# A GEGLU feed-forward kernel: x block 1 by DMA transpose instead of TensorE, the early weights issued by ScalarE, a shorter warm-up, and another split of the first bank copies

## The chip, the core and the metric

The kernel runs on one core of a Trainium2 chip. The metric is the device time of one execution in microseconds (us). An execution is timed from outside; the span of a profile is 1.3 to 1.6 us shorter. One core is used, so there is no second die to compare with.

## The reference

```python
B, S, D, F = 32, 32, 1024, 3584          # 1024 rows of x, bf16
out = (gelu_tanh(x @ w_gate) * (x @ w_up)) @ w_down
```

## The kernel before

The bulk of the kernel is a Strassen-like arrangement of 128x512 matmuls, in a stream that TensorE runs almost without a break (busy 268.2 of 270.8 us). The change touches only the first 16 us, where the first eight tiles of h = gelu(x wg) * (x wu) are made for the first 512 rows of x. That stage works in *blocks* of 128 rows of the contraction (block 0 to 7). For the first four tiles ("quad 0") it does blocks 0 and 1, then moves the eight half-done PSUM banks away (`kept`), does the second four tiles ("quad 1"), and comes back. j = 0 is the gate weight, j = 1 the up weight. (The DMAs load x and the weights into SBUF. A PSUM bank takes the 128x512 sums that a row of matmuls adds up; the kernel reuses it once VectorE or ScalarE has copied it out. In the trace of before the last of these copies on VectorE ends at 10.43 us, and its bank is reused at 10.55.)

The kernel holds x transposed in SBUF (`xT`). Blocks 0 and 1 are loaded as they are (`xn`) and transposed on TensorE. Blocks 2 to 7 come by transposing DMAs from SyncE.

```python
for n in [512] * 6 + [P] * 2:                       # warm-up on constants
    mm(3, one[:, 0:P], one[:, 0:n], True, True)
NX = 2
for i, eng in enumerate(("sp", "act")):             # x blocks 0 and 1, as they are
    dma(eng, xn[:, 2*i:2*i+2, :], x_r[:, 2*i:2*i+2, 0:NX*P], 0, f"xn{i}")
# ... load_quad(eng, q, j, k0, k1): weight blocks k0..k1 of quad q, half j
for q in range(2):
    for k in range(NX):
        load_quad("sp", q, 0, k, k + 1)
        load_quad("act", q, 1, k, k + 1)
for k0, k1 in ((2, 3), (3, 4), (4, 5), (5, 6), (6, 8)):
    pr.add("sp", "dma_start_transpose", xT[0][:, k0:k1, :], xf[0:512, k0*P:k1*P], ...)
for k in range(2, 4):
    for j in range(2):
        load_quad("act", 1, j, k, k + 1)
act(warm[:, 0:1], const0, GELU, 0)                  # makes ScalarE load its table
for k in range(NX):                                 # TensorE transposes, VectorE copies out
    ...
for k in range(NX):                                 # quad 0, blocks 0 and 1: matmuls 0 to 15
    for j in range(2):
        for m in range(4):
            raw(m, j, k, 2*m + j, k == 0)           # bank 2m+j
            if k == NX - 1:
                copy(("act", "dve")[m % 2], kept[m][:, j, :], bank(2*m + j), ...)
for i, k in enumerate((4, 6)):                      # blocks 4..7 of quad 1, after those copies
    for j in range(2):
        load_quad("act", 1, j, k, k + 2, 9 + i)
# ... matmuls 16 on: quad 1, blocks 0 to 5, each block 4 gate then 4 up matmuls
```

Below, *matmul n* is the n-th matmul on real data. Matmul 0 is block 0, matmul 8 block 1, matmul 16 the first of quad 1, which reuses the bank of matmul 8; matmul 48 begins block 4 of quad 1.

Of the kernel before, what the change touches and what calls it, by code (L numbers as in the profile page):

```python
# [6 lines left out]
P = 128  # L7
BF16 = mybir.dt.bfloat16
# [115 lines left out]
def bass_standalone__geglu_ffn__sampling_kernel(  # L124
# [11 lines left out]
    DK, FM = D // P, F // P  # L136
# [3 lines left out]
    x_r = xf.rearrange("(tc p) d -> p tc d", p=P)  # L140
# [3 lines left out]
    pr = _Program()  # L144

    with ExitStack() as es:
        def sb(name, shape, dtype):
            return es.enter_context(nc.sbuf_tensor(name, shape, dtype))

        hT = sb("hT", [P, FM, N], BF16)  # L150
# [5 lines left out]
        ident = sb("ident", [P, P], BF16)  # L156
        warm = sb("warm", [P, 2], FP32)
        p1 = sb("p1", [P, 512], FP32)
        ps = es.enter_context(nc.psum_tensor("ps", [P, 8, 512], FP32))
        const0 = nc.const_aps.tensor(0.0, [P, 1], FP32)  # L160

        xT = [arena[:, a:a + 4096].rearrange("p (k n) -> p k n", n=512) for a in (16384, 0)]
        quad = [arena[:, a:a + 8192].rearrange("p (j k c) -> p j k c", j=2, k=DK) for a in (20480, 8192)]
        def duo(a): return arena[:, a:a + 4096].rearrange("p (j k c) -> p j k c", j=2, k=DK)
        wd = [[arena[:, a:a + 7168].rearrange("p (k n) -> p k n", n=512) for a in row] for row in ((0, 7168), (14336, 21504))]
        xn = hT[:, FM - 1, :].rearrange("p (t c) -> p t c", c=2 * P)
        Sf = S[:, :, :].bitcast(FP32)
        Tf = T[:, :, :, :, :].bitcast(FP32)
        T2r = T[:, :, :, :, :].rearrange("p u j k c -> p (u j k c)").rearrange("p (s n) -> p s n", n=512)
# [9 lines left out]
        def mm(bank, lhsT, rhs, start, stop, held=False, add=False):  # L179
            return pr.add("pe", held_matmul if held else "matmul", ps[:, bank, 0:rhs.shape[-1]], lhsT, rhs,  # L180
                          start=start, stop=stop, skip_group_check=add)
# [4 lines left out]
        def act(out, a, f, at):  # L186
            return pr.add("act", "activation", out, a, f, at=at)

        def dma(eng, out, a, at, name, after=()):
            return pr.add(eng, "dma_start", out, a, at=at, dma=name, after=after)  # L190
# [6 lines left out]
        pr.add("pool", "memset", ident[:, :], 0.0)  # L197
        pr.add("pool", "affine_select", ident[:, :], ident[:, :], [[-1, P]], ALU.not_equal, 1.0,
               base=0, channel_multiplier=1)
        for n in [512] * 6 + [P] * 2:  # L200
            mm(3, one[:, 0:P], one[:, 0:n], True, True)

        NX = 2
        for i, eng in enumerate(("sp", "act")):
            dma(eng, xn[:, 2 * i:2 * i + 2, :], x_r[:, 2 * i:2 * i + 2, 0:NX * P], 0, f"xn{i}")

        def load_quad(eng, q, j, k0, k1, at=0, after=()):
            dma(eng, quad[q][:, j, k0:k1, :], w_r[j][:, k0:k1, 4 * q * P:4 * (q + 1) * P], at, f"w{q}_{j}_{k0}", after)

        for q in range(2):  # L210
            for k in range(NX):
                load_quad("sp", q, 0, k, k + 1)
                load_quad("act", q, 1, k, k + 1)
        for k0, k1 in ((2, 3), (3, 4), (4, 5), (5, 6), (6, 8)):
            pr.add("sp", "dma_start_transpose", xT[0][:, k0:k1, :], xf[0:512, k0 * P:k1 * P], dma=f"x{k0}_0")
        for k in range(2, 4):
            for j in range(2):
                load_quad("act", 1, j, k, k + 1)
        act(warm[:, 0:1], const0, GELU, 0)
        for k in range(NX):  # L220
            for i, b in enumerate((6, 7) if k == 0 else (4, 5)):
                half = ps[:, b, 0:P].bitcast(BF16)
                for t in range(2):
                    pr.add("pe", "transpose", half[:, t * P:(t + 1) * P], xn[:, 2 * i + t, k * P:(k + 1) * P], ident[:, :])
                pr.add("dve", "tensor_copy", xT[0][:, k, i * 256:(i + 1) * 256], half)



# [3 lines left out]
        def piece(a): return a.rearrange("p t n -> p (t n)").bitcast(FP32).rearrange("p (j n) -> p j n", j=2)  # L232
        kept = [piece(hT[:, m:m + 2, :]) for m in (14, 16, 18, 20, 22, 24, 26, 10, 12)] + [piece(o11[:, :, :])]
# [10 lines left out]
        bank = lambda b: ps[:, b, :]  # L244

        def copy(eng, out, a, at):
            if eng == "act":
                act(out, a, COPY, at)
            else:
                pr.add("dve", "tensor_copy", out, a, at=at)  # L250
# [3 lines left out]
        def raw(m, j, k, b, start):  # L254
            return mm(b, quad[m // 4][:, j, k, m % 4 * P:(m % 4 + 1) * P], x0[:, k, :], start, k in (NX - 1, 3, DK - 1), add=not start and k >= NX)
# [6 lines left out]
        for k in range(NX):  # L262
            for j in range(2):
                for m in range(4):
                    raw(m, j, k, 2 * m + j, k == 0)
                    if k == NX - 1:
                        copy(("act", "dve")[m % 2], kept[m][:, j, :], bank(2 * m + j), 6.5 + 0.9 * j + 0.1 * m)
        for i, k in enumerate((4, 6)):
            for j in range(2):
                load_quad("act", 1, j, k, k + 2, 9 + i)  # L270
# [376 lines left out]
```

## Time and profile before

| what | where it is read | value |
|---|---|---|
| median time | timed runs | 272.03 us (271.36 to 272.37) at first, 272.09 with three more |
| TensorE busy, span | page, part 1 | 268.2 of 270.8 us |
| first matmul on data | timeline | 4.61 us |
| spacing of matmuls of 512 columns | trace, start to start | 0.427 us until 6.67 us, 0.216 us after |
| last of the bank copies on VectorE ends | trace | 10.43 us, its bank is reused at 10.55 |

The chain of waits of before, in order of time (start, length, what; the count after x is of instructions):

```profile
by line: PE ps L117 99.0%; DVE o L117 0.1%; issue 0.0%
...
0.77 3.79 PE ps L117 x16
4.56 0.05 issue
4.61 264.41 PE ps L117 x1190
```

TensorE bounds the kernel from 0.77 to 269.02 us. Until then nothing else is on the chain for more than 0.05 us, and after it only a last VectorE instruction of 0.29 us. So a change to the start is worth what it does to the TensorE stream and nothing more.

The timeline of TensorE's weight loads in before shows two rates. "The clock switches" means in this document that the spacing of the matmuls falls from 0.427 to 0.216 us. That a clock does it is my reading and not shown: the clock column of the windows view is 1.00 on both sides (before, 4 to 6 and 8 to 10 us). At the slow rate every load stands on a line of its own, 0.43 us apart; at full rate they merge into one line (start, length, engine, source line, operation, tiles, shape, count, idle time before and what ended it):

```profile
3.39 0.90 PEld L117 LDWEIGHTS ps<-ident,hT 128*128 128x128 bf16 x8
4.58 0.14 PEld L117 LDWEIGHTS ps<-arena 128*128 128x128 bf16 x2 [0.29 <-issue]
4.99 0.15 PEld L117 LDWEIGHTS ps<-arena 128*128 128x128 bf16 x1 [0.28 <-DVE arena L117]
5.42 0.15 PEld L117 LDWEIGHTS ps<-arena 128*128 128x128 bf16 x1 [0.28 <-issue]
5.84 0.15 PEld L117 LDWEIGHTS ps<-arena 128*128 128x128 bf16 x1 [0.28 <-issue]
6.27 0.15 PEld L117 LDWEIGHTS ps<-arena 128*128 128x128 bf16 x1 [0.28 <-issue]
6.67 3.55 PEld L117 LDWEIGHTS ps<-arena 128*128 128x128 bf16 x17 [0.25 <-issue]
10.48 0.38 PEld L117 LDWEIGHTS ps<-arena 128*128 128x128 bf16 x3 [0.27 <-DVE hT L117]
```

The bank copies on VectorE in before, from its timeline. They are four, and two alternate with two on ScalarE in each half:

```profile
7.95 2.48 DVE L117 COPY hT<-ps 128x512 f32<-128x512 f32 x4 [3.06 <-PE ps L117]
```

Four stretches of before in the windows view. The columns are the stretch, its length, the busy time of PE, PEld, DVE, ACT and POOL with their instructions, the granted clock, the DMA engines' busy share and their GB/s:

```profile
18.00:20.00 2.00, 2.00 (x11) 0.88 (x9) 0.00 (x0) 0.00 (x0) 0.00 (x0) 1.00 1.10 349
22.40:23.40 1.00, 1.00 (x6) 0.49 (x5) 0.97 (x3) 1.00 (x3) 0.00 (x0) 1.00 1.28 287
22.40:25.40 3.00, 3.00 (x15) 1.37 (x14) 2.97 (x6) 3.00 (x7) 0.00 (x0) 1.00 1.11 163
8.00:12.00 4.00, 4.00 (x20) 1.80 (x19) 2.43 (x4) 1.79 (x4) 0.00 (x0) 1.00 1.13 202
```

From 18 to 20 us only plain weight loads move data (349 GB/s), and from 8 to 12 us both plain loads and transposing DMAs do (202 GB/s). From 22.4 to 25.4 us only transposing DMAs do: the last plain load before had landed at 22.39, the next was issued at 25.69. They moved 287 GB/s in the first of these three microseconds (DMA share 1.28), 149 in the second (share 1.54) and 52 in the third (share 0.52, so part of that time the engines had nothing to do): 163 over all three.

### The profile page before, as it was taken

The numbers are of one execution on the slowest core, as the hardware profiler recorded it, in microseconds if no ns is written. First come the engines' busy times: TensorE is split into PE (matmuls) and PEld (weight loads), VectorE is DVE, ScalarE is ACT, GpSimd is POOL, SyncE is SP. The second block draws the span as 40 slices with busy tenths as digits, with TensorE's granted clock in tenths as the row PEclk, the third lists the DMA queues.
The fourth block names the chain that finished last, engine by engine and source line by source line (L and its number), as shares of the span: only waits on it lengthen the run. The fifth ranks groups of instructions, "written<-read, shape, count | busy, mean of one in ns | idle before, by whom it ended". The sixth has DMA issues, their size and how long they took to land.

```text
span 270.8 us, 3333 instructions
## 1 busy us (share of the span) xinstructions
PE 268.2 (99%) x1206; PEld 192.6 (71%) x1206; DVE 208.2 (77%) x246; ACT 136.1 (50%) x221; POOL 37.1 (14%) x23
## 2 busy tenths in 40 slices
PE   8999999999999999999999999999999999999997
PEld 4444448888888888888776776674458888888884
DVE  1338998998899889988764739379976999999921
ACT  2339877566756675667455554531220305057452
POOL 1000003123302330233344160000000000000000
DMA  6999970050492002971900070294010000002102
GB/s 205 205 316 204 280 188 4 13 141 0 116 291 60 0 0 80 254 251 51 263 0 0 0 247 27 65 351 129 0 39 19 4 0 0 0 0 80 58 21 97
DMA packets 45024, 27.47 MB, mean 101 GB/s; under 512 B 8656, under 2 KB 45008, under 8 KB 45008
## 3 DMA queue, kind: packets, MB, share of 16 engines
q1 hardware_dynamic: 42496, 25.04, 34.0%
q10 hardware_dynamic: 2512, 2.23, 3.3%
q8 instruction: 9, 0.15, 0.2%
q14 instruction: 7, 0.06, 0.1%
HBM read 23.33 MB, written 2.10 MB: 94 GB/s over the span
## 4 chain that ended last, share of the span: by engine, by line
PE 99%; DVE 0%; issue 0%
PE ps L117 99%; DVE o L117 0%
## 5 line engine op out<-in xcount | busy, mean ns | idle before, releaser
L117 PE MATMUL ps<-S,T 128*128 128x512 f32 x560 | 129.2, 391 | 0.0
L117 PEld LDWEIGHTS ps<-S,T 128*128 128x128 f32 x560 | 105.2, 188 | 22.3
L117 ACT ACTIVATE tmp<-ps 128x512 f32<-128x512 f32 x64 | 38.0, 596 | 51.7 <-PE ps L117 51.5
L117 POOL TENSOR_TENSOR T<-arena 128x1024 fp32r<-128x1024 bf16 x17 | 36.4, 2153 | 124.5 <-PE ps L117 81.7
L117 PE MATMUL ps<-T,S 128*128 128x512 f32 x224 | 51.3, 390 | 0.0
L117 DVE TENSOR_TENSOR T<-arena,T 128x1024 fp32r<-128x1024 bf16 x42 | 51.0, 1220 | 0.2
L117 PEld LDWEIGHTS ps<-T,S 128*128 128x128 f32 x224 | 42.1, 188 | 8.8
L117 ACT ACTIVATE ps<-ps 128x512 f32<-128x512 f32 x44 | 25.6, 584 | 37.0 <-PE ps L117 37.0
L117 DVE TENSOR_TENSOR hT<-tmp,ps 128x512 bf16<-128x512 f32 x56 | 37.0, 684 | 8.7 <-PE ps L117 6.7
L117 PE MATMUL ps<-arena 128*128 128x512 bf16 x192 | 43.5, 385 | 0.1
L117 DVE TENSOR_TENSOR tmp<-ps,tmp 128x512 f32<-128x512 f32 x28 | 19.4, 692 | 23.5 <-PE ps L117 23.5
L117 PEld LDWEIGHTS ps<-arena 128*128 128x128 bf16 x192 | 18.5, 99 | 23.7 <-issue 2.4
L117 DVE TENSOR_TENSOR T<-arena 128x1024 fp32r<-128x1024 bf16 x25 | 30.0, 1222 | 4.4 <-PE ps L117 4.3
L117 DVE TENSOR_TENSOR ps<-ps,tmp 128x512 f32<-128x512 f32 x32 | 22.3, 696 | 3.0 <-PE ps L117 3.0
L117 PE MATMUL ps<-arena,hT 128*128 128x512 bf16 (+2 forms) x126 | 24.6, 356 | 0.0
L117 PEld LDWEIGHTS ps<-arena,hT 128*128 128x128 bf16 x126 | 11.7, 98 | 12.7 <-issue 0.5
L117 ACT ACTIVATE tmp<-tmp 128x512 f32<-128x512 f32 x28 | 17.6, 632 | 2.4 <-DVE tmp L117 2.1
L117 ACT ACTIVATE ps<-hT 128x512 f32<-128x512 f32 x22 | 13.0, 599 | 7.6 <-DVE hT L117 7.6
L117 DVE TENSOR_TENSOR S<-hT 128x1024 fp32r<-128x1024 bf16 x14 | 16.6, 1221 | 0.0
L117 ACT ACTIVATE T<-arena 128x1024 fp32r<-128x1024 bf16 x14 | 14.8, 1059 | 0.0
L117 ACT ACTIVATE hT<-ps 128x512 f32<-128x512 f32 x18 | 9.5, 602 | 7.0 <-PE ps L117 7.0
L117 PE MATMUL ps<-S 128*128 128x512 f32 x56 | 12.9, 389 | 0.0
(33 smaller groups left out, 94.4 us busy)
## 6 DMA issues: line engine op xcount, KB each, us to landing
arena<-in_w_down_dram SPq DMA_DIRECT2D x4, 1792.0 KB, 9.4
arena<-in_w_gate_dram SPq DMA_DIRECT2D x10, 512.0 KB, 4.8
arena<-in_w_up_dram SPq DMA_DIRECT2D x10, 512.0 KB, 5.9
out_dram<-arena SPq DMA_DIRECT2D x12, 128.0 KB, 1.7
arena<-in_w_up_dram ACTq DMA_DIRECT2D x6, 128.0 KB, 5.6
arena<-in_w_gate_dram SPq DMA_DIRECT2D x3, 256.0 KB, 6.3
arena<-in_w_up_dram SPq DMA_DIRECT2D x3, 256.0 KB, 6.5
arena<-in_w_gate_dram SPq DMA_DIRECT2D x4, 128.0 KB, 5.1
```

The source lines that it names most:

```text
L117: ins = name(eng, *args, **kw) if callable(name) else getattr(eng, name)(*args, **kw)
```

## The change

The intent is to begin sooner. TensorE transposes only block 0, so the two x loads halve (64 KB each; they landed in before at 3.25 and 3.46) and four transposes go. Block 1 comes by the first transposing DMA. To make room on SyncE's queue, ScalarE issues nearly all early weights, block by block, gate and up in turn. The warm-up shrinks from six matmuls of 512 columns and two of 128 to five and one. ScalarE is then busy issuing for longer (its last early issue ended at 5.23 in before), so five of the eight bank copies go to VectorE.

```diff
-        for n in [512] * 6 + [P] * 2:
+        for n in [512] * 5 + [P]:
...
-            dma(eng, xn[:, 2 * i:2 * i + 2, :], x_r[:, 2 * i:2 * i + 2, 0:NX * P], 0, f"xn{i}")
+            dma(eng, xn[:, 2 * i:2 * i + 2, :], x_r[:, 2 * i:2 * i + 2, 0:P], 0, f"xn{i}")
...
-        for q in range(2):
-            for k in range(NX):
-                load_quad("sp", q, 0, k, k + 1)
-                load_quad("act", q, 1, k, k + 1)
-        for k0, k1 in ((2, 3), (3, 4), (4, 5), (5, 6), (6, 8)):
+        load_quad("sp", 0, 0, 0, 1)
+        load_quad("act", 0, 1, 0, 1)
+        for q, k0, k1 in ((0, 1, 2), (1, 0, 1), (1, 1, 2), (1, 2, 4)):
+            for j in range(2):
+                load_quad("act", q, j, k0, k1)
+        for k0, k1 in ((1, 2), (2, 3), (3, 4), (4, 5), (5, 6), (6, 8)):
             pr.add("sp", "dma_start_transpose", xT[0][:, k0:k1, :], ...)
-        for k in range(2, 4):
-            for j in range(2):
-                load_quad("act", 1, j, k, k + 1)
...          # the TensorE transposes: block 0 alone, banks 6 and 7
-                        copy(("act", "dve")[m % 2], kept[m][:, j, :], ...)
+                        copy("act" if (m, j) in ((3, 0), (1, 1), (3, 1)) else "dve", kept[m][:, j, :], ...)
```

More of the change, by code (lines that the diff above doesn't have):

```diff
@@ L165, in bass_standalone__geglu_ffn__sampling_kernel @@
         wd = [[arena[:, a:a + 7168].rearrange("p (k n) -> p k n", n=512) for a in row] for row in ((0, 7168), (14336, 21504))]
-        xn = hT[:, FM - 1, :].rearrange("p (t c) -> p t c", c=2 * P)
+        xn = hT[:, FM - 1, 0:4 * P].rearrange("p (t c) -> p t c", c=P)
         Sf = S[:, :, :].bitcast(FP32)
@@ L204, in bass_standalone__geglu_ffn__sampling_kernel @@
         for i, eng in enumerate(("sp", "act")):
-            dma(eng, xn[:, 2 * i:2 * i + 2, :], x_r[:, 2 * i:2 * i + 2, 0:NX * P], 0, f"xn{i}")
+            dma(eng, xn[:, 2 * i:2 * i + 2, :], x_r[:, 2 * i:2 * i + 2, 0:P], 0, f"xn{i}")
         def load_quad(eng, q, j, k0, k1, at=0, after=()):
             dma(eng, quad[q][:, j, k0:k1, :], w_r[j][:, k0:k1, 4 * q * P:4 * (q + 1) * P], at, f"w{q}_{j}_{k0}", after)
-        for q in range(2):
-            for k in range(NX):
-                load_quad("sp", q, 0, k, k + 1)
-                load_quad("act", q, 1, k, k + 1)
-        for k0, k1 in ((2, 3), (3, 4), (4, 5), (5, 6), (6, 8)):
+        load_quad("sp", 0, 0, 0, 1)
[4 more added lines that the diff above has]
+        for k0, k1 in ((1, 2), (2, 3), (3, 4), (4, 5), (5, 6), (6, 8)):
             pr.add("sp", "dma_start_transpose", xT[0][:, k0:k1, :], xf[0:512, k0 * P:k1 * P], dma=f"x{k0}_0")
-        for k in range(2, 4):
-            for j in range(2):
-                load_quad("act", 1, j, k, k + 1)
         act(warm[:, 0:1], const0, GELU, 0)
-        for k in range(NX):
-            for i, b in enumerate((6, 7) if k == 0 else (4, 5)):
-                half = ps[:, b, 0:P].bitcast(BF16)
-                for t in range(2):
-                    pr.add("pe", "transpose", half[:, t * P:(t + 1) * P], xn[:, 2 * i + t, k * P:(k + 1) * P], ident[:, :])
-                pr.add("dve", "tensor_copy", xT[0][:, k, i * 256:(i + 1) * 256], half)
+        for i in range(2):
+            half = ps[:, 6 + i, 0:P].bitcast(BF16)
+            for t in range(2):
+                pr.add("pe", "transpose", half[:, t * P:(t + 1) * P], xn[:, 2 * i + t, :], ident[:, :])
+            pr.add("dve", "tensor_copy", xT[0][:, 0, i * 256:(i + 1) * 256], half)
         NP, EARLY = 14, 10
@@ L266, in bass_standalone__geglu_ffn__sampling_kernel @@
                     if k == NX - 1:
-                        copy(("act", "dve")[m % 2], kept[m][:, j, :], bank(2 * m + j), 6.5 + 0.9 * j + 0.1 * m)
+                        copy("act" if (m, j) in ((3, 0), (1, 1), (3, 1)) else "dve", kept[m][:, j, :], bank(2 * m + j), 6.5 + 0.9 * j + 0.1 * m)
         for i, k in enumerate((4, 6)):
```

## The prediction

> **What bounds the kernel now.** TensorE. The page gives PE 268.2 us of a 270.8 us span, and the chain of waits is PE from 0.77 us to 269.0 us almost without a break. In the timeline, matmuls of 512 columns start every 0.427 us until 6.67 us and every 0.216 us afterwards (the fp32 products of the bulk every 0.226 us). After 6.67 us I find only about 16 gaps, under 2 us together. So the change can touch only what stands before the stream reaches full rate, plus any new gap it makes. [...] no run here shows yet what moves the switch.
>
> **Before, in the timeline.** Warm-up 0.77 to 3.50, eight transposes 3.50 to 4.35 (0.107 each), VectorE copies 3.95 to 4.89 (0.29 each), first real matmul 4.61. Five real matmuls run at the slow rate, the rest at 0.216. Matmul 8 (block 1) starts at 7.32, matmul 16 (second four tiles) at 9.04.
>
> **Removed.** One warm-up matmul of 512 and one of 128 columns (0.53 us), four transposes (0.43 us), two copies. The x pieces halve, so they should land about 0.25 us earlier than 3.25 and 3.46. Block 0 is still bound by x landing, then transpose, then copy: the last transpose at about 3.3, plus the 0.79 us from transpose to matmul seen before, gives a first matmul near 4.08, some 0.5 us earlier. If the clock still switches near 6.6 us, that half microsecond is slow time: worth only about 0.26 us of stream.
>
> **Added: one transposing DMA for block 1.** SyncE issues it at about 1.75 (before, the first such issue took 1.21 us). Block 1 is needed near 7.1. Before, the first one ran from about 6.3 to 10.2 beside weight traffic, the later one alone took about 2 us. From data at about 3.2 that puts landing between 5 and 7.2: mostly hidden; I allow 0.2 us on average.
>
> **Moved: bank copies.** Before, VectorE and ScalarE each empty four banks; on VectorE one takes 0.68 us, started every 0.60 us, the first 0.42 us after its matmul starts. The last ends at 10.43, and its bank is reused at 10.55: no slack. After, VectorE has five, three of them first. Counted from matmul 8: copies end at +1.11, +1.71, +2.30, +2.90, +3.50; their banks are wanted at +1.73, +1.94, +2.16, +2.59, +3.02. So a new wait of about 0.5 us on TensorE around 9 to 10.5 us, all on the critical path.
>
> **Weights.** ScalarE issues the second tiles' blocks earlier in one queue; total bytes are equal. The tightest landing before is block 4 (15.47 against use at 15.95, 0.5 us slack); the same copies release it, so I expect it to hold.
>
> **Sum.** -0.26 (start) +0.5 (bank copies) +0.2 (block 1) = about +0.4: 272.4 us, 80% range 271.4 to 273.6. Faster by over 2%: 0.3%; within 2%: 98.2%; slower by over 2%: 1.5%.
>
> **What would show it.** First matmul on x near 4.1; a gap or rate change at the same 6 to 7 us; the waits view with PE or its weight load waiting for VectorE's bank copies around 9 to 10.5; block 1's landing before about 7; full rate from there to the end with the same gaps.
>
> **What would make it wrong.** The clock switching at another time [...]. Block 1 landing late behind weights. If TensorE waits for w block 1 anyway, the copies' wait hides under that. If the bank copies are no limit, the result is about 271.7.

Two passages are cut from it: a description of how the clock switches, and, from what would make it wrong, the cause and the size that it gave for a switch at another time. No trace or run of this case shows them. Neither is a term of the sum, which stands whole: -0.26 + 0.5 + 0.2 = +0.44, taken as about +0.4 on the 272.03 us of before.

## The result, and the profile after

After: 272.65 us median of 6 runs (272.31 to 273.30). Before, in the same rounds: 272.09 us median of 6. The ratio is 1.0028, 95% interval 1.0010 to 1.0046. A ratio here is the mean time of one kernel's runs over that of the other's runs of the same rounds, so it is not quite the ratio of the medians. The interval lies above 1, so it is slightly slower.

The chain of waits of after. It no longer begins on TensorE:

```profile
by line: PE ps L117 93.3%; DMA arena<-in_w_gate_dram 2.8%; ACTq L117 2.0%; ACT L117 0.5%; ACT hT L117 0.3%; issue 0.2%; DVE o L117 0.1%; ACT warm L117 0.1%
...
6.38 1.28 ACT L117
...
7.88 0.77 ACT hT L117 x2
8.65 7.61 DMA arena<-in_w_gate_dram
16.27 0.05 issue
16.32 253.12 PE ps L117 x1142
```

Read from the bottom: matmul 48 at 16.32 us waited for the gate weights of block 4. These landed at 16.27 after 7.6 us, and were issued at 8.65 by ScalarE, which until then had issued loads, loaded its table (6.38) and copied banks. Before had no such wait.

The weight loads of after:

```profile
3.19 0.15 PEld L117 LDWEIGHTS ps<-ident,hT 128*128 128x128 bf16 x1
4.16 0.13 PEld L117 LDWEIGHTS ps<-arena 128*128 128x128 bf16 x2 [0.82 <-DMA arena<-in_w_gate_dram]
4.56 0.15 PEld L117 LDWEIGHTS ps<-arena 128*128 128x128 bf16 x1 [0.28 <-issue]
4.99 1.01 PEld L117 LDWEIGHTS ps<-arena 128*128 128x128 bf16 x5 [0.28 <-issue]
6.69 1.88 PEld L117 LDWEIGHTS ps<-arena 128*128 128x128 bf16 x10 [0.69 <-issue]
9.08 0.11 PEld L117 LDWEIGHTS ps<-arena 128*128 128x128 bf16 x2 [0.50 <-DVE hT L117]
9.74 0.13 PEld L117 LDWEIGHTS ps<-arena 128*128 128x128 bf16 x2 [0.55 <-issue]
10.27 0.55 PEld L117 LDWEIGHTS ps<-arena 128*128 128x128 bf16 x4 [0.41 <-DVE hT L117]
```

The first matmul came at 4.16 instead of 4.61. In this execution the clock had already switched at 5.2 us. At 6.72 matmul 8 had waited for block 1 of x, which landed at 6.59 (the line names no releaser; the weights of matmul 8 had landed at 4.76). At 9.08, 9.74 and 10.27 stand the waits for banks that VectorE was still emptying (the line at 9.74 names none either; the fourth copy ended at 9.62, and the weights had landed at 7.91). Its copies and the DMA rate in after:

```profile
7.14 3.08 DVE L117 COPY hT<-ps 128x512 f32<-128x512 f32 x5 [3.21 <-PE ps L117]
```

```profile
4.00:12.00 8.00, 7.49 (x30) 2.76 (x31) 3.08 (x5) 2.96 (x5) 0.00 (x0) 1.00 1.16 206
18.00:20.00 2.00, 2.00 (x11) 0.88 (x9) 0.00 (x0) 0.00 (x0) 0.00 (x0) 1.00 1.10 346
```

The starts of the same matmuls in the two traces give the whole account of the two profiled executions (us; the difference is after minus before):

| stretch | before | after | difference | what it is |
|---|---|---|---|---|
| start to matmul 0 | 4.606 | 4.160 | -0.446 | earlier start |
| 0 to 8 | 2.709 | 2.564 | -0.145 | clock switched earlier (-0.536), wait for x block 1 (+0.391) |
| 8 to 16 | 1.726 | 1.723 | 0.00 | |
| 16 to 40 | 5.180 | 5.726 | +0.546 | bank copies: gaps at matmuls 18, 20, 22 |
| 40 to 64 | 5.180 | 5.638 | +0.458 | late weights of block 4: 0.415 at matmul 48 |
| 64 to end | 249.603 | 249.606 | 0.00 | |
| TensorE's end | 269.004 | 269.417 | +0.413 | |

The wait of 0.391 is the 0.607 us from matmul 7 to matmul 8, less the regular 0.216.

The rows add up, but they are not separate causes. By the chain, matmul 48 began at 16.32 because block 4 landed at 16.27. Without the gaps of the copies TensorE would have come to matmul 48 half a microsecond sooner and, had the landing stayed the same, waited half a microsecond longer there. So in this execution the copies were not on the chain that set the end, although the prediction has their wait "all on the critical path".

One trace is one execution, though. The moment of the clock's switch differs by several microseconds between the profiled executions (full rate from 4.12 us or sooner in k11, from 10.26 in k4), so the experiments were timed as well.

### The profile page after: what moved, and what is told of

It reads as the page before. It is cut to its first block, busy times and chain, and to the rows that moved or that the text cites. A ratio compares the mean times of both kernels' runs of the same rounds, so it can differ in the third digit from the quotient of the medians.

```text
span 271.2 us, 3318 instructions
## 1 busy us (share of the span) xinstructions
PE 267.5 (99%) x1200; PEld 191.3 (71%) x1200; DVE 208.4 (77%) x245; ACT 135.6 (50%) x220; POOL 37.1 (14%) x23
## 4 chain that ended last, share of the span: by engine, by line
PE 93%; DMA 3%; ACTq 2%; ACT 1%; issue 0%; DVE 0%
PE ps L117 93%; DMA arena<-in_w_gate_dram 3%; ACTq L117 2%; ACT L117 0%; ACT hT L117 0%; DVE o L117 0%; ACT warm L117 0%
## 5 line engine op out<-in xcount | busy, mean ns | idle before, releaser
L117 PEld LDWEIGHTS ps<-arena 128*128 128x128 bf16 x192 | 17.9, 98 | 25.6 <-issue 2.8
```

The costliest lines, as they stand in the source:

```text
L117: ins = name(eng, *args, **kw) if callable(name) else getattr(eng, name)(*args, **kw)
```

## The experiments

Theory at the outset: the change starts TensorE 0.45 us sooner; the five serial copies on VectorE take 0.5 us back; waits for data and for the clock take the rest. Rivals: the gaps at 18 to 22 are late data whoever copies; the clock's moment has nothing to do with TensorE's idle time; block 1 of x alone is the cause.

A summary first. "Full rate from" is the first matmul start at the 0.216 us spacing in the one profiled execution. The waits are the gaps beyond the regular spacing in that execution. The kernel before was run 42 more times beside them, on four chips: 271.32 to 272.41 us, medians 271.60 to 271.87.

| run | median us (range) | ratio to before (95%) | full rate from | waits of TensorE in its trace |
|---|---|---|---|---|
| before | 272.09 (271.36 to 272.37) | | 6.67 | none |
| after | 272.65 (272.31 to 273.30) | 1.0028 (1.0010, 1.0046) | 5.25 | x block 1 0.39, copies 0.5, block 4 0.42 |
| k1 even copies | 272.38 (271.96 to 273.23) | 1.0024 (1.0007, 1.0041) | 6.87 | up weights of block 2 0.29 |
| k2 before, split copies | 272.36 (271.89 to 272.93) | 1.0018 (1.0005, 1.0031) | 5.01 | copies 0.5 |
| k3 block 4 early | 272.42 (271.91 to 272.82) | 1.0019 (1.0007, 1.0031) | 4.97 | x block 1 1.21, copies 0.5 |
| k4 even copies, table early | 273.04 (272.16 to 273.92) | 1.0037 (1.0014, 1.0060) | 10.26 | none |
| k5 after, filler | 272.53 (272.08 to 272.67) | 1.0029 (1.0015, 1.0043) | 5.61 | x block 1 0.12, copies 0.5, block 4 0.1 |
| k6 before, block 1 turned late | 272.04 (271.93 to 272.23) | 1.0011 (0.9997, 1.0025) | never | see below |
| k7 warm-up of 3 | 273.00 (272.72 to 273.11) | 1.0044 (1.0030, 1.0059) | 8.66 | copies 0.2 |
| k8 even copies, filler | 272.47 (271.74 to 272.86) | 1.0022 (1.0006, 1.0039) | 6.51 | none |
| k9 even, filler, table early | 272.06 (271.39 to 272.55) | 1.0013 (0.9998, 1.0029) | 5.62 | up weights of block 2 0.39 |
| k10 before, short warm-up | 272.28 (271.64 to 273.33) | 1.0020 (1.0003, 1.0037) | 5.81 | none |
| k11 no wait for x block 1 | 272.26 (271.80 to 273.70) | 1.0024 (1.0005, 1.0044) | 4.12 or sooner | weights 0.33, 0.12, 0.78, copies 0.2 |
| k12 k9 with fine blocks | 272.41 (272.11 to 272.52) | 1.0024 (1.0010, 1.0038) | 6.43 | block 4 0.12 and 0.44 |

For k6 the median, range and ratio are of its four fast executions. All others gave right results; k11 is wrong on purpose. The traces of k5, k6, k7, k8 and k12 lack nine matmul records each; the regular gaps of 0.43 us that this leaves are not counted as waits.

### k1: the even copies put back into after

```diff
-    copy("act" if (m, j) in ((3, 0), (1, 1), (3, 1)) else "dve", kept[m][:, j, :], ...)
+    copy(("act", "dve")[m % 2], kept[m][:, j, :], ...)
```

> The kernel after, with the bank copies dealt out evenly again (four to VectorE, four to ScalarE). Theory (five copies in a row on VectorE hold TensorE): the 0.20, 0.24 and 0.08 us gaps before matmuls 18, 20 and 22 go from VectorE; but ScalarE's table load now ends at 7.67 and its warm-up at 7.88, so its first copy starts about 0.65 us late and ends at about 8.4, 8.9, 9.35 and 9.8, against wants of about 8.45, 8.88, 9.3 and 9.75: some 0.2 us of gaps come back, now put down to ScalarE. Net 0.3 us less than after in the trace. Rival (the gaps are late weights or x, whoever copies): the same three gaps stay, about 0.5 us. Block 4's gap (matmul 48) stays at about 0.4 us in both.

The gaps at 18, 20 and 22 are gone from the trace. The expected 0.2 us on ScalarE did not appear, because here the clock switched at 6.8 us and TensorE was later, so that ScalarE's first copy, at 7.78, was early enough. Block 4 landed at 15.38 and made no gap; the wait that I expected to stay is thus not a fixed cost of the queue order. A wait at matmul 36 came instead: the up weights of block 2 landed at 13.38. The median is 0.27 us under that of after, but the two were timed in different jobs and the intervals overlap.

### k2: only the copy split, on before

```diff
-    copy(("act", "dve")[m % 2], kept[m][:, j, :], ...)
+    copy("act" if (m, j) in ((3, 0), (1, 1), (3, 1)) else "dve", kept[m][:, j, :], ...)
```

> The kernel before, with only the copy split of the change (five to VectorE, three of them first). Theory: about 0.5 us of new gaps on TensorE before matmuls 18, 20 and 22 (0.2, 0.2 and 0.1), all data landing as before, and 0.5 us more in the trace's end than the kernel before at the same clock switch (about 272.6). Rival (late data makes those gaps in the kernel after): no gap here, time as before, 272.1.

The weight loads of k2 show the waits for VectorE where after has them:

```profile
5.01 3.37 PEld L117 LDWEIGHTS ps<-arena 128*128 128x128 bf16 x16 [0.24 <-DVE arena L117]
8.88 0.11 PEld L117 LDWEIGHTS ps<-arena 128*128 128x128 bf16 x2 [0.50 <-DVE hT L117]
9.54 0.13 PEld L117 LDWEIGHTS ps<-arena 128*128 128x128 bf16 x2 [0.55 <-issue]
10.07 0.76 PEld L117 LDWEIGHTS ps<-arena 128*128 128x128 bf16 x5 [0.41 <-DVE hT L117]
```

The gaps beyond regular spacing are 0.20, 0.24 and 0.08 us at matmuls 18, 20 and 22, the same three numbers as in after, although x and the weights come in before's order. (The line at 9.54 names no releaser: the fourth copy ended at 9.42, matmul 20 began at 9.57.) The median rose by 0.49 us (272.36 against 271.87), the ratio is 1.0018. This part is shown, on before: five copies in a row on VectorE, one begun every 0.60 us and 0.68 us long, cost about 0.5 us. The rival (late data) has fallen for these gaps.

### k3: block 4 of the weights issued early, on after

```diff
-    load_quad("act", 1, j, k, k + 2, 9 + i)
+    load_quad("act", 1, j, k, k + 2, 9 + i if i else 0)
```

> The kernel after, with ScalarE issuing blocks 4 and 5 of the second tiles' weights right behind blocks 2 and 3 (at about 6.3 us) instead of after its bank copies (8.66). Theory (the weights stand behind the last transposing DMA, which SyncE begins to issue at 8.2 and which takes 2.7 us): the first of them lands by about 14.5 instead of 16.27, the 0.42 us gap before matmul 48 goes, and x blocks 6 and 7 land later than 16.9 but before their use at 19.8. Rival (the engines are simply slow while transposes and plain loads mix): it lands at about 16 again and the gap stays at 0.3 us or more, or block 4 of x becomes late. The table load moves about 1.1 us later, so ScalarE's first copy (8.28 in after) is at about 9.0 and may add up to 0.3 us.

The gate weights of block 4 landed at 15.00 (expected by 14.5, 16.27 in after), and the gap at 48 went; matmul 48 itself came 0.3 us later than in after, which helped. But in this execution block 1 of x landed at 7.34 us, and the clock had switched before 5 us, so the wait moved to matmul 8:

```profile
4.16 2.27 PE L117 MATMUL ps<-arena 128*128 128x512 bf16 x8 [0.56 <-DMA arena<-in_w_gate_dram]
7.47 9.77 PE L117 MATMUL ps<-arena 128*128 128x512 bf16 x42 [1.04 <-DMA arena<-in_x_dram]
```

The time, 272.42 us, cannot be told from that of k1 or k2.

### k4: even copies, and the table load moved up

```diff
     for q, k0, k1 in ((0, 1, 2), (1, 0, 1), (1, 1, 2), (1, 2, 4)):
+        if (q, k0) == (1, 0):
+            act(warm[:, 0:1], const0, GELU, 0)      # and removed below; with k1's edit
```

> The kernel after, with even copies and the table load moved ahead of the last six weight issues on ScalarE (at about 2.8 us instead of 6.4). Theory: ScalarE is free when block 1's first bank is done, so no gap at matmuls 16 to 23 (less than 0.1 us), 0.5 us better there than after. If the table load holds ScalarE's issue stream, its six weight loads start about 1.5 us later and the gaps come back as late weights at matmul 16 (blocks 0 and 1 of the second tiles) or 32; if it doesn't, they issue as in after. Rival (copies don't matter): gaps of 0.5 us stay.

The table load (2.76 to 4.04 us) did not hold ScalarE's issues: the next one went out at 2.82. No copy gap is left, but with TensorE at the slow rate until 10.26 that tests little; k9 has the same copies and table load at full rate from 5.62, and shows no copy gap either. The six runs fell into two groups, 272.16 to 272.39 and 273.69 to 273.92. The profiled run (273.77) is of the upper one, and its weight loads show why:

```profile
4.39 0.13 PEld L117 LDWEIGHTS ps<-arena 128*128 128x128 bf16 x2 [1.05 <-DMA arena<-in_w_gate_dram]
4.79 0.15 PEld L117 LDWEIGHTS ps<-arena 128*128 128x128 bf16 x1 [0.28 <-issue]
...
9.91 0.15 PEld L117 LDWEIGHTS ps<-arena 128*128 128x128 bf16 x1 [0.28 <-issue]
10.26 0.53 PEld L117 LDWEIGHTS ps<-arena 128*128 128x128 bf16 x3 [0.20 <-issue]
```

TensorE stood idle for 1.0 us between its last transpose and matmul 0, since the gate weights of block 0 landed only at 4.35, and the slow rate lasted until 10.2 us. That made a new theory: idle time of TensorE ahead of matmul 0 delays the clock's switch. The idle microsecond and the late switch stand in one trace; that the one made the other, and how, it does not show.

### k5 and k8: throw-away matmuls in the idle stretch

k5 is after, k8 is k1, each with

```diff
+    for n in range(5):                               # behind the transposes of block 0
+        mm(3, one[:, 0:P], one[:, 0:P], True, True)
```

> The kernel after, with five throw-away matmuls of 128 columns behind the four transposes, which fill the time in which TensorE waits for the copies (3.4 to 4.1 us). Theory [...]: the slow tail of after (272.3 to 273.3) and of the even-copies runs (two at 273.2, three at 273.7 to 273.9) goes, all runs within about 0.8 us, median about 272.3, and the profile's switch lies between 4.5 and 7.5 us. Rival [...]: the same spread as after, a run or two over 273, median 272.6.

> The kernel after with even bank copies and the five throw-away matmuls. Theory: the 273.2 us mode of the even-copies run goes, all runs 271.7 to 272.4, median about 272.0, equal to before: the earlier start (0.45 us of slow time, worth 0.25) is then given back by the waits for block 1 of x and for late weights (0 to 0.5 us). Rival (copies and clock explain nothing): 272.4 with a tail over 273.

To test: TensorE's idle stretch delays the switch in part of the executions (theory), or has nothing to do with it (rival).

k5 lost its slow tail as expected (highest 272.67 against 273.30), but its median, 272.53, is nearer the rival's. k8's profile has no wait at all and ends sooner than before's (TensorE at 268.60 against 269.00), yet three of its six runs lie at 272.7 to 272.9: my expected 272.0 failed. Both profiled executions were the fastest of their kernel. With the gap filled no run is over 273, and the rest stays where it was.

### k6: before, with block 1 turned on TensorE after four matmuls

x blocks 0 and 1 come as separate plain loads, block 1 behind the first weights; its transposes go between matmuls 3 and 4, in one bank; with the short warm-up and the throw-away matmuls.

```diff
-    dma(eng, xn[:, 2*i:2*i+2, :], x_r[:, 2*i:2*i+2, 0:NX*P], ...)
+    dma(eng, xn[:, 2*i:2*i+2, 0:P], x_r[:, 2*i:2*i+2, 0:P], ...)
...
                 load_quad("act", q, 1, k, k + 1)
+                if q == k == 0:
+                    ...                  # the same for block 1, from sp and act
...
             for j in range(2):
+                if k == 0 and j == 1:
+                    turn(1, (7, 7), 1)   # four transposes into bank 7, two copies
```

> The kernel before (its queues and its even copies), with x blocks 0 and 1 loaded as separate plain loads, block 1 turned on TensorE after the first four matmuls of block 0, the shorter warm-up, and the five throw-away matmuls. This takes the early start of the change without the transposing DMA. Theory: first matmul at about 4.1 as in after, no wait of 0.4 to 1.2 us for block 1 at matmul 8, no copy gaps: 0.2 to 0.5 us under before (271.4 to 271.7). If block 1's plain load or the weights, each queued behind one more load, come late, a wait at matmul 4 to 12 of up to 0.5 us gives it back (272).

Four runs gave 271.93 to 272.23 us, ratio 1.0011 (0.9997 to 1.0025): no gain. The fifth, the profiled one, took 557.7 us. It is slow from end to end: matmuls of 512 columns start every 0.443 us or so throughout, at about every fifth step 0.55 us, while the profile says that the clock was granted in full (the 1.00 ahead of the DMA share):

```profile
20.00:40.00 20.00, 20.00 (x44) 6.40 (x43) 5.53 (x8) 4.57 (x9) 0.00 (x0) 1.00 1.08 232
200.00:220.00 20.00, 20.00 (x45) 12.57 (x44) 8.34 (x11) 7.29 (x12) 2.13 (x1) 1.00 0.30 80
```

In before the stretch 200 to 220 holds 91 matmuls, here 45. I saw this once in some 120 executions of all kernels and can't say whether it has to do with k6. Because of it, the fast runs of k6 have no trace, and why they gain nothing is not settled by this run.

### k7 and k10: less warm-up

k7 is after with `[512] * 3` as warm-up; k10 is before with the change's `[512] * 5 + [P]`.

> The kernel after with three warm-up matmuls of 512 columns instead of five and a half: TensorE then stands idle from about 2.0 to 2.9 us as well. First matmul unchanged at about 4.1 (x binds). Theory (idle time of TensorE delays the clock's switch): more executions switch late; times rise, most of them to 273 to 274, the profile's switch probably at 7 to 10.5 us. Rival [...]: times and spread as after, 272.3 to 273.3.

> The kernel before with only the shorter warm-up of the change (five matmuls of 512 columns and one of 128). x still lands at about 3.25 and 3.46, so the first matmul comes at about 4.4 instead of 4.6. Theory of my prediction (each 0.1 us of earlier start in slow time is worth half): 0.1 us under before, 271.8, hardly to be told from it. Rival (block 1 of the weights, which lands at 6.2 to 6.9 in the two profiles with these queues, holds matmul 8 whenever the clock switches early, so an earlier start is worth nothing): as before, 271.9. [...]

k7 was slower than after in its runs (272.72 to 273.11, 1.0044), with the first matmul at 4.03 and full rate only from 8.66. The late switch in its trace speaks against the rival (the moment of the switch does not depend on TensorE). The times do not decide it: I had expected most runs at 273 to 274, and three of four lie at 273.00 to 273.11, but all four lie inside the range of after, and the intervals of the ratios overlap. k10 did not gain the 0.1 us: 272.28, ratio 1.0020, with one run of six at 273.33. In its trace x landed at 3.65, so matmul 0 came at 4.60, as in before: the shorter warm-up only put idle time where warm-up had been. Its median fits the branch that is cut from the expectation for what it said of the clock (above 272.2 if the idle stretch costs time), and its ratio (1.0003 to 1.0037) is as far from 1 as that of the copy split in k2. Where the time went is not seen: the profiled execution was a quick one (271.91), switched at 5.81 and has no wait.

### k9: k8 with the early table load

> The even-copies-and-filler kernel with the table load issued at about 2.8 us, so that ScalarE is free before the first bank is done. Theory (the even-copies kernels are still 0.2% over before because, where the clock switches early, ScalarE's first copy waits for the table load until 7.9 us, and because block 1 of x is awaited): the part of ScalarE goes, median about 272.1 (0.1% over before), the upper runs of 272.8 become 272.4. Rival (the rest is block 1 of x and late weights alone): unchanged, 272.4 to 272.5. [...]

The sentence cut from it expected no run near 273.8 if the throw-away matmuls keep the switch from coming late, and such runs, as in k4, if they don't.

272.06 us, ratio 1.0013, the best of the change's order. k9 and k4 differ only in the five throw-away matmuls: 271.39 to 272.55 against 272.16 to 273.92, no run near 273.8 against three of six. The gain over k8 (0.4 us of median) has the expected sign, but the two ran on different chips and the intervals overlap. The remaining wait in its profile is at matmul 36: up weights of block 2, landed at 12.87.

### k11: after without the wait for block 1 of x

```diff
+    kx = 0 if (k == 1 and m < 4) else k               # wrong result on purpose
-    mm(b, quad[...], x0[:, k, :], ...)
+    mm(b, quad[...], x0[:, kx, :], ...)
```

> The kernel after, but the eight matmuls of block 1 of the first tiles read x block 0 (a wrong result on purpose; the transposing DMA of block 1 still runs, only nobody waits for it so early). Theory (block 1 of x holds TensorE where the clock switches early: 0.4 us in the profile of after, 1.2 in the w4-early run, none where it switches after 6.3): the lower half of the runs gains up to 0.5 us, the median 0.2 to 0.3 us: about 272.3 against 272.65. Matmul 8 then waits for the weights of block 1 alone, which land at 6.3 to 6.7, so the gain is small if they come as late as x. Rival (no part): 272.65.

This is the most telling trace. The clock was fast from matmul 0 on, and nobody waited for block 1 of x (it landed at 7.22). Matmul 8 started at 5.84, almost 0.9 us before after's. And all was given back: waits at 16 (gate weights of quad 1, landed 7.85), 20 and 22 (copies; for 20 the profile names the up weights, but these landed at 8.66 and the fourth copy ended at 8.74, 0.15 us before the matmul), 32, and 36 (up weights of block 2, landed 13.30):

```profile
7.89 0.11 PEld L117 LDWEIGHTS ps<-arena 128*128 128x128 bf16 x2 [0.66 <-DMA arena<-in_w_gate_dram]
...
9.39 0.98 PEld L117 LDWEIGHTS ps<-arena 128*128 128x128 bf16 x6 [0.38 <-DVE hT L117]
...
13.34 0.55 PEld L117 LDWEIGHTS ps<-arena 128*128 128x128 bf16 x4 [1.11 <-DMA arena<-in_w_up_dram]
```

TensorE ended at 269.02, level with before's 269.00, in which the clock had switched more than 2 us later. The median, 272.26, is 0.39 under that of after, in another job; the ratio, 1.0024 against 1.0028, does not separate them.

### k12: k9 with blocks 2 and 3 issued singly

```diff
-    for q, k0, k1 in ((0, 1, 2), (1, 0, 1), (1, 1, 2), (1, 2, 4)):
+    for q, k0, k1 in ((0, 1, 2), (1, 0, 1), (1, 1, 2), (1, 2, 3), (1, 3, 4)):
```

> The even-copies, throw-away-matmuls, early-table kernel, with blocks 2 and 3 of the second tiles' weights issued one block at a time (as in before) instead of two at a time. Theory (the two-block pieces make the up weights of block 2 land with those of block 3, at 12.7 to 13.9 us in all runs of this order against 9.1 to 10.1 in before, so that matmul 36, wanted near 12.5 to 13, waits 0.3 to 0.8 us in three profiles): they land at about 11.3, no gap at 36, median 0.1 to 0.3 us lower than 272.06, at 271.8 to 271.9 level with before. Rival (the engines, not the piece size, set that landing): still 12.7 or later and the gap stays where the clock switches early. Two more issues on ScalarE cost it 1 us, which the early table load leaves free.

The up weights of block 2 landed at 11.83 instead of 12.87 and the wait at 36 went. The piece size is part of the cause, then. But block 4 came later, the up half at 16.89, and the wait came up again there:

```profile
14.64 2.02 PE L117 MATMUL ps<-arena 128*128 128x512 bf16 x8
16.94 1.25 PE L117 MATMUL ps<-arena 128*128 128x512 bf16 x5 [0.28 <-DMA arena<-in_w_up_dram]
```

272.41 us, ratio 1.0024: no gain. None of the versions beats before.

## Why the prediction was right, and where a step of it was not

The predicted 272.4 us and the range 271.4 to 273.6 hold the measured 272.65. The sum was right in sign; two of its terms, and two assumptions, were not. That the two traces differ by 0.41 us, just as the predicted +0.4, is luck. The start (-0.45 for -0.26) and the wait for block 1 (+0.39 for +0.2) missed by 0.19 us in opposite directions, and two terms that the sum did not have, the clock's earlier switch (-0.54) and the late block 4 (+0.42), nearly cancelled.

- **"First matmul near 4.08."** It came at 4.16 (4.03 to 4.39 in the other runs of the change's order). Right.
- **"Worth only about 0.26 us of stream"**, if the clock still switched near 6.6. In the profiled pair it did not: the start gave 0.45 us and an earlier switch another 0.54. Over the traces full rate began anywhere from 4.1 to 10.3 us, so this was no number to fix. An early switch was also worth less than it seemed, since TensorE then met data that had not landed (k11).
- **"Bank copies: a new wait of about 0.5 us at 9 to 10.5 us."** Measured 0.546 in the trace of after, the same gaps in before when given the split alone (k2), and 0.49 us of its median. The size was right, and it is the best supported part. "All on the critical path" was not right for the profiled execution: there block 4 set the time of matmul 48, and the copies' gaps lay in its shadow. Undone in after (k1) the split brought about 0.3 us or less, which fits that, though two jobs with overlapping intervals don't show it. I had warned that the copies' wait would hide under a wait for data, but named another block of weights.
- **"Block 1 lands between 5 and 7.2; I allow 0.2 us."** It landed at 6.1 to 7.3 in ten traces. The wait was 0.39 in after, 1.21 in k3, 0.12 in k5, and none where the clock switched after 6.3, or in k9, where x had landed by 6.12. The size of the term depends on the clock, so it is an average at best.
- **"The tightest landing is block 4 ... I expect it to hold."** This step failed in the trace of after: block 4 landed at 16.27 instead of 15.47, 0.42 us too late, although it was issued 0.38 us sooner than in before. I had argued from equal total bytes. It is no fixed cost of the change: of the nine profiles of the change's order that issue block 4 in its place, three have a wait there (after, k5, k12) and six have none, with the gate weights landing at 14.25 to 15.38. Why it comes late where it does is not shown. From 4 to 12 us the ten kernels with the change's order moved 191 to 220 GB/s, mean 207; before, k2 and k10, with the old order, 219, 251 and 237. That fits data that come later in general, but a low rate does not go with a late block 4: it landed at 14.91 in k11 (192 GB/s) and at 15.84 in k5 (220). A tempting reading is that transposes beside plain loads slow each other: 202 GB/s together in before, against 349 for plain loads and 287 for a transpose in its best microsecond. The traces do not bear this out. With no plain load in flight, the transposes of before moved 149 GB/s in the next microsecond with the engines just as busy, and over the like stretches of 2.2 to 3.2 us in the 13 fast traces the mean rate was 157 to 247. So 202 is not below what transposes do by themselves, and no run changed the mixture, or the timing of the transposes, alone.
- **"The clock switching at another time."** The size that I gave this risk rested on nothing that the traces show. The risk is seen: k4's upper group is 1.5 us over its lower one. Of the 30 executions in the change's order with idle time and without filler (after, k1, k3, k4, k11), 7 took over 273 us; of 22 with the throw-away matmuls (k5, k8, k9, k12) none took over 272.86; of 48 of before none over 272.41. By chance alone, 0 of 22 would come up in some 1.5% of cases. So idle time of TensorE ahead of matmul 0 probably delays the switch in some executions. It is not quite shown: the limit of 273 was chosen afterwards, the pairs that differ in the filler alone (after and k5, k1 and k8, k4 and k9: 6 of 18 over 273 against 0 of 17) ran in different jobs, only one execution well over 273 was profiled (k4's, switch at 10.26), and in k11 0.7 us of idle time went with full rate from matmul 0 on. It would explain the tail, not the median: with the tail gone, k5 and k8 are still 0.2 to 0.3% over before.

What the remainder is: in the traces the early stage is held now by the clock, now by the copies, now by data that land up to 17 us. Where an edit took one wait away (k1, k11, k12), another stood in the trace, and no time came below that of before. Which share of the remaining 0.1 to 0.2% is ScalarE's later table load and which is the data can't be told: one profiled execution for each kernel and a spread of 0.4% between executions are too little. It stays open. So does the shorter warm-up: on before alone (k10) it cost about as much as the copy split alone (k2), and no run gave after its full warm-up back.

## What to carry to other kernels

Before moving a start earlier, look up when each later operand lands: an earlier TensorE may only wait for them, as here: k11 began matmul 8 almost 0.9 us before after did, waited for weights and bank copies, and ended level with before (269.02 against 269.00 us); the slack of block 4 in before, with the DMA engines' busy share at 1.12 from 4 to 12 us, was 0.5 us (landed at 15.47, used at 15.95). When serial copies free the banks that the next tiles need, count copy period against bank reuse; here one more copy on the same engine, 0.60 us after the one before it, cost 0.5 us on before, which could be computed to a tenth from its trace. Ask of every wait whether a later one covers it, as block 4 did here. Do not take idle time of TensorE during the warm-up for free: shortening the warm-up alone cost 0.2% here (k10). And where executions differ by the moment of a clock switch, look at the spread of the times and not at one profile.
